# Moving the query transposes of an attention loop to other places, two weight transposes to an earlier place, and two loads to an earlier step

## The chip, the core and the metric

The kernel runs on one core of one Trainium2 chip. TensorE (PE) multiplies and transposes, with its weight loads (PEld) running beside it; VectorE (DVE), ScalarE (ACT) and GpSimd (POOL) do the elementwise work, and SyncE (SP) issues most DMA transfers; ACT issues some as well. The metric is the device time of one execution in microseconds (us), as the median of several runs. The profile is one further execution, taken by the hardware profiler.

## The reference

The reference computes the forward output of one transformer-like block and the gradients of all eight inputs, for 2 batches of 4000 tokens with 144 channels, in bf16. One branch is attention with one head, the other a gated convolution with 5 taps:

```python
xa = _layernorm(x, axis=-1)
q, k, v = split(einsum('btd,de->bte', xa, w_qkv))
p = softmax(einsum('btd,bsd->bts', q, k) * D ** (-0.5))
glob = einsum('btd,de->bte', einsum('bts,bsd->btd', p, v), w_att_out)
h = gelu(einsum('btd,de->bte', xa, w_mlp_in));  u, g = split(h);  g = _layernorm(g)
gc[t] = sum_i g[t + i - 2] * dw_csgu[i]          # 5 taps
loc = einsum('btd,de->bte', u * gc, w_mlp_out)
m = concat(glob, loc);  m[t] += sum_i m[t + i - 2] * dw_merge[i]
out = x + einsum('btc,cd->btd', m, w_merge)
...
_out, _vjp = jax.vjp(_f, x, w_qkv, ..., w_merge);  _grads = _vjp(grad_out)
```

## The kernel before

The two batches run one after the other. Each goes through three stages; the function names are those of the code.

**Head** (`phase_head`). Tokens come as 32 blocks of 128, in 8 groups of 4. Normalised tokens are transposed into `xaT`. For batch 0 the weights are made ready first: `Weights.heads`, then `Weights.keys`. `Weights.turn` (L1128 to L1142) transposes one weight by PE through a PSUM tile `pt` (four transposes for 144 by 144) and copies it out with two DVE copies. `heads` turns the value weight, makes the tap scales, forms the product `w_voT` and turns the output weight `w_l_s` (`w_lT`). `keys` turns the query and key weights (`w_qT`, `w_kT`) and forms their product `W.M1`. Then `taps` (DVE, L1244 and L1248) and `taps1` (POOL, L1252) scale copies of `w_voT` and `w_lT` into `w_A` and `w_Bz`. `Norm.stats`, `power`, `shift` and `apply` (L1399 to L1432) normalise a group of tokens, by DVE, POOL, DVE, and then ACT and POOL.

**Attention** (`phase_attn`). It runs over 32 rows `i` of 128 queries and, for each, four column pairs `c2` of 1000 keys. Everything here is issued in the order in which the code writes it. For each `c2`:
- `unit` (L1985, L1989) forms scores `pS` for this pair and the gradient products `pD` for the pair before it; ACT takes the exponential of `pS` (L1997), DVE forms `Sm` from `pD` (L1999).
- Then come two *places*, 0 and 1. Place 0 begins with `yz` (L2035), 16 matmuls for the row two back. Each place may have X fills and ends with at most one step of the planner on PE.

An X fill (`xfill`, L2057 and L2058) is a set of 12 matmuls that adds the contribution of two rows (a row pair) to three key blocks. It needs one PSUM bank, which it gives back once the sum is taken out: by DVE for even fills (`acc`, L2073), by ACT and POOL for odd ones (`xs`, L2069 and L2070). There are 11 fills for a row pair, and the table `fills` says at which place each stands. Counted over the 16 places of a row pair, from slot 0 to slot 15, it says: slot 1 does the first halves of fills 0 and 1, and slot 2 the second halves, so that these two hold a bank each from slot 1 to slot 2. Fill 2 stands at the beginning of slot 3, fills 3 to 5 at slots 5, 6 and 7, fills 6 to 10 at slots 9 to 13.

X fills and the planner's steps draw from the same three banks (`Banks`, L1698 to L1716). The next tile always takes the bank that has been closed or handed out longest ago and is not held; if it has not been emptied yet, the writing engine waits.

The planner (`Steps`, L1719 to L1770) holds generators for the convolution branch (`pair(p)`, one for two blocks, and `wgrad(p)`) and for the query transposes (`jit(g)`, one for a group of four rows). A generator yields the kind of its next piece, how many places must pass first, and what else must have been done. Pieces of kind `V` (no PE work) are issued at every place when they are ready, within a budget. Of the ready pieces with PE work only one is issued at a place, the one that has been due longest. Kind `P` is taken at any place; kind `L` is known to the planner too, but no generator of this kernel yields it. The PE pieces are:
- `ph`: two matmuls (L1809, L1810), twice for each pair, taken out by two ACT instructions.
- `put` (L1665, L1667), four transposes, taken out by ACT, and `conv` (L1693, L1694), twelve matmuls, taken out by ACT. Each runs once for `gnC` and once for `dgC`.
- `jit` (L1954 to L1966): POOL collects a small tile `QB`, and then three steps follow, each with four transposes into `pj` (L1965) and one ACT copy (L1966). Their results are the weights of the matmuls of `unit` for the next four rows. A `jit` is started 16 places before its rows, which is slot 0.

**Tail** (`phase_tail`). It runs over `h` from 0 to 20. At even `h`, `turn` transposes, `put` (L2183) stores the last 16 channels into two DRAM tap tensors, and `fill(g)` (L2177 to L2180) reads 80 rows of taps of group `g` back into `r` with two DMAs issued by ACT (L1647). `out_mm(p)` (L2218, L2219) needs these for `p = 2g` and `2g + 1`; it runs at `h = p + 5`. At `h = 15` `spill_ef` takes four banks of sums out, in batch 0 by ACT copies (L2277 to L2279); from `h = 16` on `gr_part` (L2289) uses two of these banks. DMAs signal through eight counters, which are handed out in the order of the program over both issuing engines; a DMA waits for the one that had its counter before.

```python
due = [t for t in self.tasks if t[1] is not None and
       (t[1][0] == 'P' or t[1][0] == 'L' and self.now % 2) and self._ready(t)]
if due:
    self._step(min(due, key=lambda t: t[0]))
self.now += 1
```

Of the kernel before, what the change touches and what calls it, by code (L numbers as in the profile page):

```python
# [14 lines left out]
D = 144  # L15
# [1045 lines left out]
NGR = 8  # L1061
# [59 lines left out]
class Weights:  # L1121
# [94 lines left out]
    def heads(self, pst, ps, stats):  # L1216

        W, tp_, nc = self.W, self.tmp, self.k.nc
        cw = self.cw
        self.WvT = self.turn(W.Wqkv, D, 2 * D, D, "w_vT", pst)  # L1220
        stats()
        pt = pst.tile([128, 3, 16], BF, tag="tp", name="pt")
        for n_ in range(3):
            nc.tensor.transpose(pt[:, n_, 0:5], cw[0:5, n_ * D:n_ * D + 128], W.ident[0:5, 0:5])
            nc.tensor.transpose(pt[0:DR, n_, 6:11], cw[0:5, n_ * D + 128:n_ * D + D], W.ident[0:5, 0:5])
        nc.vector.tensor_copy(W.wm[:, :, 0, :], pt[:, 0:2, 0:5])
        nc.vector.tensor_copy(W.wm[0:DR, :, 1, :], pt[0:DR, 0:2, 6:11])
        nc.vector.tensor_scalar(W.wm[:, :, :, 2], W.wm[:, :, :, 2], 1.0, None, op0=ALU.add)
        wr = self.wr = tp_.tile([128, 2, 2, 5], F32, name="w_wr")
        nc.vector.tensor_copy(wr[:], W.wm[:, :, :, ::-1])  # L1230
        nc.vector.tensor_copy(self.wcf[:, 0, :], pt[:, 2, 0:5])
        nc.vector.tensor_copy(self.wcf[0:DR, 1, :], pt[0:DR, 2, 6:11])
        self.WvoT = self.pads.pop("w_voT")
        self.vo(ps, self.WvoT, W.Wo, self.WvT)
        WlT = self.turn(self.Wl, D, 0, D, "w_lT", pst)
        self.UT = [self.WvoT, WlT]
        self.A = [tp_.tile([128, 2, 5, D], BF, name="w_A%d" % h) for h in range(2)]
# [17 lines left out]
    def keys(self, pst, ps):  # L1255

        W, tp_, nc = self.W, self.tmp, self.k.nc
        c = float(D) ** -0.5
        WqT = self.WqT = self.turn(W.Wqkv, D, 0, D, "w_qT", pst)
        WkT = self.WkT = self.turn(W.Wqkv, D, D, D, "w_kT", pst)  # L1260
        WqTz = self.pads.pop("w_qTz")
        nc.vector.tensor_copy(WqTz[:, :, 112:128], WqT[:, :, 128:D])
        W.M1 = self.k.wp.tile([128, 2, D], BF, name="w_M1")
        self.fused(ps, lambda kt: WqT[:, kt, :], self.two(WkT), c, 0, 128, W.M1[:, 0, :])
        self.fused(ps, lambda kt: WqTz[:, kt, :], self.two(WkT), c, 0, 128, W.M1[:, 1, :])
# [357 lines left out]
class Taps:  # L1623


    L = 2 + NBK * 128 + 2
# [92 lines left out]
class Steps:  # L1719
# [36 lines left out]
    def place(self, tensor=True):  # L1756

        self.left = min(self.left + self.rate, self.most)
        again = True
        while again:  # L1760
            again = False
            for t in sorted(self.tasks, key=lambda t: t[0]):
                if (t[1] is None or t[1][0] == 'V') and self._ready(t):
                    self._step(t)
                    again = True
        if tensor:
            due = [t for t in self.tasks if t[1] is not None and (t[1][0] == 'P' or t[1][0] == 'L' and self.now % 2) and self._ready(t)]
            if due:
                self._step(min(due, key=lambda t: t[0]))
        self.now += 1  # L1770
# [165 lines left out]
def phase_attn(k, W, b, S):  # L1936
# [3 lines left out]
    with ExitStack() as es:  # L1940
# [6 lines left out]
        P, Sm = S.P, S.Sm  # L1947
# [7 lines left out]
        def jit(g):  # L1955
            r = slice(g * 4, g * 4 + 4)
            jt[g] = [xp.tile([128, 4, 128], BF, tag=t_, name=t_) for t_ in ("QTm", "BTm", "QBr")]
            for off, src in ((0, S.Q_t), (32, S.B_t), (64, S.Q_t), (96, S.B_t)):
                nc.gpsimd.tensor_scalar(QB[:, :, off:off + DR], src[:, r, 128:D], 1.0, 0.0, op0=ALU.mult, op1=ALU.add)
            for step in range(3):  # L1960
                yield 'P', 2
                src = (S.Q_t[:, r, 0:128], S.B_t[:, r, 0:128], QB[:])[step]
                pj = ps_f.tile([128, 4, 128], BF, tag="f", name="pj")
                for j in range(4):
                    nc.tensor.transpose(pj[:, j, :], src[:, j, :], id_[:])  # L1965
                nc.scalar.copy(jt[g][step][:], pj[:])  # L1966
# [145 lines left out]
def phase_tail(k, W, b, S, nrm, nxt):  # L2112
# [3 lines left out]
    with ExitStack() as es:  # L2116
# [33 lines left out]
        def load_dh(g):  # L2150
            nc.sync.dma_start(dh[g // 2][:, g % 2 * 4:g % 2 * 4 + 4, :], S.dh_d[:, g * 4:g * 4 + 4, :])
# [25 lines left out]
        def fill(g):  # L2177
            for h in range(2):
                r_ = G["r", h, g] = wk.tile([128, 512], BF, tag="r80_%d" % h, name="r80")
                taps[h].load(r_[0:80, :], g * 512, 512, nc.scalar)  # L2180
# [27 lines left out]
        def turn_dx2(pt, hT):  # L2208
            nc.scalar.copy(hT[:], pt[:])
# [62 lines left out]
        def spill_ef():  # L2272
            if fin_:
                return fin_.ef(EF)
            EFs = pp.tile([128, 12, D], F32, name="EFs")
            for n_ in range(3):
                nc.scalar.copy(EFs[:, n_ * 3:n_ * 3 + 3, :], EF[n_][:, 0:3 * D].rearrange("p (a b) -> p a b", b=D))  # L2277
            nc.scalar.copy(EFs[:, 9:10, :], EF[3][:, 0:D].rearrange("p (a b) -> p a b", b=D))
            nc.scalar.copy(EFs[0:80, 10:12, :], EF[3][0:80, D:3 * D].rearrange("p (a b) -> p a b", b=D))  # L2279
            nc.sync.dma_start(k.A.EF_d[:, 0:10, :], EFs[:, 0:10, :])  # L2280
            nc.sync.dma_start(k.A.EF_d[0:80, 10:12, :], EFs[0:80, 10:12, :])
# [19 lines left out]
        NPR = NBK // 2  # L2301
        with tc.manual_schedule():
            loads(0)
            load_dh(0)
            load_dh(1)
            loads(1)
            rows80(0)
            prep(0)
            for h in range(NPR + 5):
                g, hf = divmod(h, 2)  # L2310
                if 0 < h < NPR:
                    turn_dx2(*turn_dx(h))
                if hf == 0 and 0 <= g - 2 < NGR - 1:
                    fill(g - 2)
                if h == NPR + 1:
                    fill(NGR - 1)
                if hf == 0 and g < NGR:
                    turn(g, 0)
                    corr(g, 0)
                    turn(g, 1)  # L2320
                    corr(g, 1)
                elif g < NGR:
                    if g:
                        corr(g, 2)
                    corr(g, 3)
                if h == 0:
                    turn_dx2(*turn_dx(0))
                    corr(0, 2)
                if hf == 1 and g + 1 < NGR:
                    rows80(g + 1)  # L2330
                if 0 <= h - 1 < NPR:
                    sums_act(h - 1)
                    sums_dve(h - 1)
                if hf == 0 and g < NGR:
                    put(g)
                if nrm:
                    for lag, f_ in ((5, nrm.apply), (4, nrm.shift), (3, nrm.power), (2, nrm.stats), (1, nrm.load)):
                        q, m = divmod(h - lag, 2)
                        if m == 0 and 0 <= q < NGR:
                            f_(q)  # L2340
                    if NPR + 2 <= h < NPR + 4:
                        narrow_go(k, nxt, h - NPR - 2, nrm.ld)
                if h == NPR - 1:
                    spill_ef()
                if fin_ and 4 <= h < NPR - 1:
                    fin_.loads(h - 4)
                if hf == 0 and g + 1 < NGR:
                    prep(g + 1)
                if 0 <= h - 1 < NPR:
                    means(h - 1)  # L2350
                if 0 <= h - 2 < NPR:
                    fin(h - 2)
                if h == NPR + 4:
                    spill_gr()
                if 0 <= h - 5 < NPR:
                    out_mm(h - 5)
                if fin_ and h == NPR + 4:
                    fin_.gr_out()
                if NPR <= h < NPR + 4:
                    for q in range(4):  # L2360
                        j = (h - NPR) * 8 + 2 * q
                        gr_part(range(j, j + 2))
                        if fin_:
                            fin_.step((h - NPR) * 4 + q)
                if h < NPR:
                    dx_mm(h)
                if hf == 0 and 0 <= g - 1 < NGR:
                    load_x(g - 1)
                if nrm and NPR - 2 <= h < NPR + 1:
                    take_go(k, nxt, 1, h - NPR + 2, nrm.ld)  # L2370
                if hf == 1 and g + 2 < NGR:
                    load_dh(g + 2)
                    loads(g + 2)
# [346 lines left out]
```

## Time and profile before

| | us |
|---|---|
| median of 7 runs | 1271.89 |
| lowest and highest | 1269.64, 1280.3 |
| the profiled execution | 1275.91 |
| its span | 1274.0 |
| PE busy / DVE / ACT / POOL | 1209.3 / 960.7 / 843.4 / 559.2 |

In the span, the head of batch 0 takes from 0 to about 48 us, its attention from 48 to about 545, its tail to about 640. Batch 1's attention begins near 658 and ends near 1155, and its tail runs to the end. Over 48 to 584 us PE is busy for 518.29 of 536 us, DVE for 418.22, ACT for 369.75, POOL for 232.97. PE's busy time counts overlapping matmuls, so that the distance from the start of one matmul to the start of the next says more: it is 0.06 us in a stream of 144 columns.

### The profile page before, as it was taken

Reading aid. Unit: us, or ns where it says so; the run is one execution under the profiler, and the core shown is the slowest. Engines: PE = TensorE matmul, PEld = TensorE weight load, DVE = VectorE, ACT = ScalarE, POOL = GpSimd, SP = SyncE. Lnnn points to the kernel's source line nnn. Section 1 sums busy time; section 2 is a strip of 40 time slices with the busy share of each in tenths; the row PEclk is TensorE's granted clock in tenths of the full one; section 3 lists DMA queues with packets and bytes.
Section 4 is the critical chain, followed back from the end, with each engine's and each line's share of the span. In section 5 each row is a group of like instructions: output and inputs, shape, how many; then the busy total and the mean of one; then the engine's idle time right before and its main releaser. Section 6 shows DMA issues by size and latency. Waiting matters only on the chain.

```text
span 1274.0 us, 39810 instructions
## 1 busy us (share of the span) xinstructions
PE 1209.3 (95%) x15118; PEld 948.8 (74%) x15118; DVE 960.7 (75%) x3261; ACT 843.4 (66%) x2494; POOL 559.2 (44%) x1007
## 2 busy tenths in 40 slices
PE   7999999999999999989999999999999999998995
PEld 4667777777777777789886777777777776778984
DVE  6567788888788787858646678888888878885674
ACT  4767777777777666556567777777767776654442
POOL 6313444454445443357512254544544445225650
PEclk9999999999999999999999999999999999999998
DMA  6479998888999999978857998999898999997861
GB/s 192 115 135 171 144 165 155 159 146 154 171 162 153 157 164 162 153 202 230 223 158 139 156 158 144 157 166 165 149 168 153 159 163 156 159 161 189 254 160 25
DMA packets 633616, 205.43 MB, mean 161 GB/s; under 512 B 576719, under 2 KB 630948, under 8 KB 633380
## 3 DMA queue, kind: packets, MB, share of 16 engines
q1 hardware_dynamic: 626912, 197.46, 82.6%
q10 hardware_dynamic: 6500, 5.32, 1.7%
q8 instruction: 120, 1.97, 0.6%
q14 instruction: 84, 0.69, 0.2%
HBM read 46.11 MB, written 21.79 MB: 53 GB/s over the span
## 4 chain that ended last, share of the span: by engine, by line
PE 69%; DVE 15%; DMA 5%; issue 4%; ACT 4%; POOL 2%; SPq 1%; ACTq 0%; DVEq 0%; POOLq 0%
PE y L2035 15%; PE pS L1989 9%; PE X L2057 8%; PE X L2058 8%; PE pD L1989 7%; DVE Sm L1999 5%; PE pS L1985 5%; PE pb L1518 3%; PE pc L1693 2%; DVE jg L1916 2%; PE po L2218 1%; DMA gs<-in_grad_out_dram 1%; PE gr L2289 1%; DVE acc L2073 1%; DMA dhr<-dh_d 1%
## 5 line engine op out<-in xcount | busy, mean ns | idle before, releaser
L1999 DVE SCALAR_TENSOR_TENSOR Sm<-pD,Pm 128x500 bf16<-128x500 f32 x512 | 325.7, 673 | 83.1 <-PE pD L1989 49.2
L1997 ACT ACTIVATE Pm<-pS 128x500 bf16<-128x500 f32 x512 | 295.9, 586 | 39.4 <-PE pS L1989 36.3
L2057 PE MATMUL X<-Qs,Sm 128*128 128x144 bf16 x2048 | 285.8, 226 | 9.3 <-DVE acc L2073 8.9
L2070 POOL TENSOR_TENSOR acc<-xs,acc 128x432 f32<-128x432 f32 x150 | 169.0, 1127 | 281.2 <-ACT xs L2069 280.8
L2058 PE MATMUL X<-Bt,Pm 128*128 128x144 bf16 x2048 | 285.6, 226 | 0.8 <-DVE Bt L2022 0.8
L2058 PEld LDWEIGHTS <-Pm 128*128 128x128 bf16 x2048 | 200.2, 98 | 11.9 <-issue 11.4
L2057 PEld LDWEIGHTS <-Sm 128*128 128x128 bf16 x2048 | 200.1, 98 | 1.6 <-issue 1.0
L2035 PEld LDWEIGHTS <-PT 128*128 128x128 bf16 x2048 | 137.3, 98 | 31.3 <-issue 3.5
L2035 PEld LDWEIGHTS <-ST 128*128 128x128 bf16 x2048 | 136.4, 98 | 27.6
L2069 ACT COPY xs<-X 128x432 f32<-128x432 f32 x150 | 78.0, 520 | 111.7 <-PE X L2058 103.0
L2073 DVE TENSOR_TENSOR acc<-X,acc 128x432 f32<-128x432 f32 x180 | 104.0, 578 | 54.1 <-PE X L2058 53.5
L1997 ACT ACTIVATION_READ_ACCUMULATOR Pm<-pS 128x1 f32 x512 | 104.8, 205 | 0.0
L1985 PE MATMUL pD<-rb,QBr 16*128 16x500 bf16 x448 | 95.7, 378 | 4.0 <-DVE Sm L1999 3.5
L1989 PEld LDWEIGHTS <-BTm 128*128 128x128 bf16 x512 | 49.9, 98 | 60.2 <-issue 2.1
L1985 PE MATMUL pS<-rb,QBr 16*128 16x500 bf16 x448 | 91.9, 379 | 0.3
L1916 DVE SCALAR_TENSOR_TENSOR jg<-gnC,dgC 128x256 bf16<-128x256 bf16 x160 | 90.0, 562 | 1.2
L2045 POOL TENSOR_TENSOR B_t<-zd,yd 128x144 bf16<-128x144 f32 x64 | 34.1, 532 | 113.3 <-ACT zd L2044 112.9
L1989 PEld LDWEIGHTS <-QTm 128*128 128x128 bf16 x512 | 29.0, 97 | 72.4 <-issue 72.4
L1989 PE MATMUL pS<-rb,QTm 128*128 128x500 bf16 x256 | 76.9, 382 | 0.0
L1989 PE MATMUL pS<-ra,QTm 128*128 128x500 bf16 x256 | 76.5, 380 | 0.0
L2035 PE MATMUL y<-ra,PT 128*128 128x144 bf16 x1024 | 74.9, 227 | 1.4 <-ACT zd L2044 1.4
L2035 PE MATMUL y<-rb,PT 128*128 128x144 bf16 x1024 | 74.3, 226 | 1.4 <-ACT zd L2044 1.4
(638 smaller groups left out, 2878.0 us busy)
## 6 DMA issues: line engine op xcount, KB each, us to landing
gs<-in_grad_out_dram SPq DMA_DIRECT2D x24, 720.0 KB
dh_d<-dh SPq DMA_DIRECT2D x32, 144.0 KB
dhr<-dh_d SPq DMA_DIRECT2D x16, 288.0 KB
gs<-in_grad_out_dram SPq DMA_DIRECT2D x8, 540.0 KB
xg<-in_x_dram SPq DMA_DIRECT2D x21, 144.0 KB
dug_d<-dug SPq DMA_DIRECT2D x16, 144.0 KB
dug<-dug_d SPq DMA_DIRECT2D x32, 72.0 KB
ug_d<-ug SPq DMA_DIRECT2D x32, 72.0 KB
```

The costliest lines, as they stand in the source:

```text
L1518: nc.tensor.matmul(pb[:], goT[:, i * 128 + m:i * 128 + m + 128], W.GL[:, m, :, :].rearrange("p a b -> p (a b)"), start=(m == 0), stop=False)
L1916: nc.vector.scalar_tensor_tensor(jg[:], a_[:, m:m + 256], 1.0, d_[:, 2:258], op0=ALU.mult, op1=ALU.mult, accum_out=dws[:, p, m:m + 1])
L1985: nc.tensor.matmul(o_[h][:, 0:SC], jt[i // 4][2][rr, i % 4, :], S.XR[c2][rr, 0:SC], start=True, stop=False)
L1989: nc.tensor.matmul(o_[h][:, 0:SC], jt[i // 4][w][:, i % 4, :], S.xaT[:, c0:c0 + SC], start=False, stop=True)
L1997: nc.scalar.activation(P[:, pb, c1:c1 + SC], o_[h][:, 0:SC], ACT.Exp, accum_out=ld8[:, 0, n_:n_ + 1])
L1999: nc.vector.scalar_tensor_tensor(Sm[:, pb, c1:c1 + SC], o_[h][:, 0:SC], 1.0, P[:, pb, c1:c1 + SC], op0=ALU.mult, op1=ALU.mult, accum_out=l ...
L2035: nc.tensor.matmul(y[:, w, :], src[:, jj, :], S.xaa[:, j, :], start=(j == 0), stop=(j == NBK - 1))
L2057: nc.tensor.matmul(X[:, jj, :], Sm[:, i % NP, j * 128:(j + 1) * 128], Qs[:, i % 4, :], start=(kk == 0 and jj == 0), stop=False, skip_group ...
L2058: nc.tensor.matmul(X[:, jj, :], P[:, i % NP, j * 128:(j + 1) * 128], Bt[:, i % 4, :], start=False, stop=(kk == 1), skip_group_check=True)
L2069: nc.scalar.copy(xs[:, 0:nj, :], X[:, 0:nj, :])
L2070: nc.gpsimd.tensor_tensor(a_, xs[:, 0:nj, :], a_, op=ALU.add)
L2073: nc.vector.tensor_tensor(a_, X[:, 0:nj, :], a_, op=ALU.add)
```

## The change

There are four edits in three groups.

1. `jit` yields its three steps as kind `L` with 1 place to pass, where they were kind `P` with 2. Kind `L` is now taken at slots 3 to 15 (`self.now % 16 > 2`), where it was at odd places.
2. The query and key weights are turned in `heads`, between the product `w_voT` and the turn of the output weight; `keys` finds them there.
3. In the tail the last two `fill`s, groups 6 and 7, stand together at `h = 15`, just before `spill_ef`. They stood at `h = 16` and `h = 17`.

```diff
@@ Weights.heads
         self.WvoT = self.pads.pop("w_voT")
         self.vo(ps, self.WvoT, W.Wo, self.WvT)
+        self.WqT = self.turn(W.Wqkv, D, 0, D, "w_qT", pst)
+        self.WkT = self.turn(W.Wqkv, D, D, D, "w_kT", pst)
         WlT = self.turn(self.Wl, D, 0, D, "w_lT", pst)
@@ Weights.keys
-        WqT = self.WqT = self.turn(W.Wqkv, D, 0, D, "w_qT", pst)
-        WkT = self.WkT = self.turn(W.Wqkv, D, D, D, "w_kT", pst)
+        WqT, WkT = self.WqT, self.WkT
@@ Steps.place
-            due = [... (t[1][0] == 'P' or t[1][0] == 'L' and self.now % 2) and self._ready(t)]
+            due = [... (t[1][0] == 'P' or t[1][0] == 'L' and self.now % 16 > 2) and self._ready(t)]
@@ jit
             for step in range(3):
-                yield 'P', 2
+                yield 'L', 1
@@ phase_tail
-                if hf == 0 and 0 <= g - 2 < NGR - 1:
+                if hf == 0 and 0 <= g - 2 < NGR - 2:
                     fill(g - 2)
-                if h == NPR + 1:
-                    fill(NGR - 1)
...
                 if h == NPR - 1:
+                    fill(NGR - 2)
+                    fill(NGR - 1)
                     spill_ef()
```

The lines below the first edit keep their order but have numbers higher by one in the profile of the changed kernel (L1965 becomes L1966, L2057 becomes L2058, and so on).

More of the change, by code (lines that the diff above doesn't have):

```diff
@@ L1766, in place @@
         if tensor:
-            due = [t for t in self.tasks if t[1] is not None and (t[1][0] == 'P' or t[1][0] == 'L' and self.now % 2) and self._ready(t)]
+            due = [t for t in self.tasks if t[1] is not None and (t[1][0] == 'P' or t[1][0] == 'L' and self.now % 16 > 2) and self._ready(t)]
             if due:
```

## The prediction

> **What bounds the kernel now.** I read the page first: busy shares, then the chain that ended last, then the costliest groups.
>
> ```profile
> PE 1209.3 (95%) x15118; PEld 948.8 (74%) x15118; DVE 960.7 (75%) x3261; ACT 843.4 (66%) x2494; POOL 559.2 (44%) x1007
> ...
> PE 69%; DVE 15%; DMA 5%; issue 4%; ACT 4%; POOL 2%; SPq 1%; ACTq 0%; DVEq 0%; POOLq 0%
> ...
> L2057 PE MATMUL X<-Qs,Sm 128*128 128x144 bf16 x2048 | 285.8, 226 | 9.3 <-DVE acc L2073 8.9
> ```
>
> PE is busy for 95% and carries 69% of the chain, so only work of PE, or waits of PE, can be gained. The last line shows such a wait: the X fills stand for 8.9 us behind DVE's sums `acc`. The chain of waits, for PE alone, gives (engine, line waited with, cause: total, times, longest):
>
> ```profile
> PE X L2057 <- DVE acc L2073: 8.9, 12, 1.7
> ...
> PE pt L1137 <- DMA w_l_s<-in_w_mlp_out_dram: 3.0, 1, 3.0
> ...
> PE ph L1809 <- ACT dgC L1669: 2.8, 2, 1.4
> ...
> PE po L2219 <- DMA r<-u: 1.9, 1, 1.9
> ...
> PE pc L1693 <- ACT gc L1867: 1.8, 2, 0.9
> ...
> PE ph L1809 <- DVE acc L2073: 1.0, 2, 0.5
> ```
>
> The lines with `acc`, `dgC` and `gc` have one cause. PE's timeline at the longest `acc` wait:
>
> ```profile
> 446.95 0.23 PE L2058 MATMUL X<-Bt,Pm 128*128 128x144 bf16 x1
> 447.01 0.39 PE L1965 MATMUL pj<-w_ident,Q_t 128*128 128x128 bf16 x4
> 449.11 0.22 PE L2057 MATMUL X<-Qs,Sm 128*128 128x144 bf16 x1 [1.71 <-DVE acc L2073]
> ```
>
> This is slot 2 of a row pair. Fills 0 and 1 hold two of the three banks until here. The `jit` step takes the third; fill 2 then gets the bank of fill 0, which ended just before. DVE empties it at 449.05 (448.45 + 0.60) because it does `Sm` (0.67 us from 447.85) first, and PE stands still.
>
> **The change part by part: the planner.** I went through all 117 PE steps of a batch, taking the excess of the gap after (or before) the step over the usual 0.06 us from start to start. `d` is the time from the last start of fill 1 to the end of fill 0's `acc`, per row pair 0.5 to 2.1 us, mean 0.92. Steps that stall fall in three classes; the other places show no stall.
>
> - Slot 2, third bank taken: `jit` 0.26, 0.54, 0.92, 0.86, 0.26, 1.87, `put` 0.56, `ph` 0.71, `conv` 0 = 5.98. The rows fit d − 0.24 for four transposes, d − 0.19 for `ph`, d − 0.66 for the longer `conv`.
> - Slot 3 with slot 2 empty: fill 2 has the third bank, the step gets that of fill 0: `ph` 0.67, `conv` 0.25 and 0 = 0.92. The rows fit d − 0.76.
> - Slots 0 and 1 both: the second step wants the bank of the first, which ACT has not emptied (the `dgC` and `gc` lines): 1.06 + 1.55 = 2.61.
>
> Together 9.51 us in batch 0 and 9.53 in batch 1; the steps of `jit` cause 4.71 of it in each.
>
> Then I ran the planner's rules by hand for the new code. The queue of steps is the same, so every step that `jit` leaves free at slots 0 to 2 is taken by `ph`, `put` or `conv`, which move up by as much as six places. The new places by number (slot = number modulo 16):
>
> - `jit` at 19, 20, 21; 51, 52, 53; 83, 87, 88; 116, 117, 119; 147, 149, 151; 179, 180, 181; 213, 214, 216: one at least at slot 3 in five of seven groups.
> - Slots 0 and 1 both: none, so 2.61 goes.
> - Slot 2: `conv` 0.43, 0.35, 0, 0, `put` 0.26, `ph` 0.61 = 1.65. `jit` has left slot 2, but others stand there.
> - Slot 3 without slot 2: `jit` 0, 0.02, 0.40, 0.14, `ph` 0.67, `conv` 0.18 and 1.34 = 2.75 (3.10 in batch 1, one `d` differs).
>
> The new sum is 4.40 and 4.75, so the gain is 5.1 + 4.8 = **9.9 us**. The steps keep their number and work, 4 transposes and one ACT copy for each `jit` step; only the cover changes. ACT's copies move with them; ACT is busy for 69% (370 of 536 us) of the attention and tail stretch. The tiles turned out here are weights of the next four rows, at least seven places later: no wait there. The DMA transposes that feed those places land at least 3.6 us before their use, more than the phase shrinks in a row pair.
>
> Bounds. Below: if none of the steps now at slots 2 and 3 costs anything (DVE early in each), the gain is the whole 9.5 per batch, 19. Above: the formulas give a new sum of about 13d − 8.3 if every `d` is alike (four `conv`, two others at slot 2, seven at slot 3). It is 9.5, no gain at all, at d = 1.37, and 19 at d = 2.1, the worst row: 19 us lost over two batches. I take the rows' own `d` for each pair, since DVE's work before fill 0's `acc` is not moved by the change.
>
> **The head.** PE stands until 8.40 for `w_l_s`, and only then turns it, and the query and key weights (8 transposes, 1.38 us). In the changed order these 8 go ahead, into the 3.04 us for which PE waits. Their four DVE copies and `w_qTz` follow, and `w_A` on DVE, at 10.68 now, could start at 9.39: at most 1.29 us earlier. But after that POOL bounds the stage:
>
> ```profile
> 9.25 1.39 POOL L1252 TENSOR_TENSOR w_A<-w_lT,w_wr 128x720 bf16<-128x720 bf16 x1 [1.97 <-DVE w_lT L1139]
> 10.73 1.17 POOL L1437 TENSOR_SCALAR g<-gs 128x320 bf16<-128x320 bf16 x1
> ...
> 13.60 1.39 POOL L1252 TENSOR_TENSOR w_A<-w_lT,w_wr 128x720 bf16<-128x720 bf16 x1
> 15.14 0.19 POOL L1413 TENSOR_SCALAR ve<-mv 128x4 f32<-128x4 f32 x1 [0.15 <-DVE mv L1406]
> ```
>
> POOL's row is full from 9.25 to 14.99, and `ve` waits only 0.15 us for DVE: if POOL's row keeps its end, 0.15 is all. But `g` takes 1.17 us while DVE does `w_A`, where elsewhere the same takes 0.46, so POOL may end earlier when DVE is done earlier. I take **−0.6**, near the middle of 0 and −1.29, as both ends are argued from rows equally near. If the weights come late, nothing is lost: they were used at the same place before.
>
> A rule that speaks against this edit: the Trainium skill, page "SBUF — State Buffer", section "Who interferes with whom", says that a DVE instruction with two SBUF inputs contends with a GpSimd instruction that reads SBUF, one locking out the other. The row of `g` (1.17 beside DVE's `w_A`, against 0.46) agrees with it. By it, moving `w_A` ahead only moves the collision onto POOL's own `w_A` at 9.25: the gain would be the 0.15 alone, and the sum smaller by 0.45.
>
> **The tail.** The edit moves four DMAs of ACT's queue (y6, u6, y7, u7) ahead of `spill_ef`. Rows of batch 0:
>
> ```profile
> 622.53 0.32 ACTq L1647 DMA_DIRECT2D r<-y  x1
> ...
> 623.11 1.33 ACT L2277 COPY EFs<-EF 128x432 f32<-128x432 f32 x3
> ...
> 625.64 0.32 ACTq L1647 DMA_DIRECT2D r<-u  x1
> ```
>
> Now y6 is issued, the five copies (1.8 us) run, and u6 goes at 625.64, held back by its counter; PE's `po` waits 1.85 us for it at 629.39. After the edit y6 to u7 come in sequence and the copies behind them. u7's counter is that of a gradient load of SP (L1107), issued at 621.31 and landed at 625.57. So ACT stands until about 625.6, and behind it stand the copies, and behind those PE's `gr`, which uses the two banks that they empty: it starts at 624.68 now and about 626.6 then, 1.9 later. Its gain is the 1.85 wait, which goes as u6 is issued earlier. SP is touched as well: its second load of the last token group takes a counter of a load that lands at 625.74 (issue now 623.61); DVE's statistics end some 2.1 us later, `og` near 630.8, ahead of `out_mm(13)` at 632.22: covered. Net −1.85 + 1.9, I take **+0.1**; ends −1.85 (PE finds `out_mm` work while `gr` waits) and +2.0 (the `po` wait stays behind other transfers). In batch 1 no wait stands at these places: 0, give or take 0.5, the largest slack missed.
>
> Sum: −9.9 − 0.6 + 0.1 = −10.4. The profiled execution takes 1275.91 us (span 1274.0) and would take 1265.5. It lies 4.0 above the median of the runs; the waits counted here don't depend on that, so the median goes from 1271.89 to **1261.5**.
>
> **The rivals.**
>
> - *The new places cost nothing* (DVE early, as at those of the 117 steps without a stall): the whole 19 goes, with 0.5 of the other edits: about 1252.5. For it: four of the new slot 3 rows are priced under 0.2. Against: `d` of 1 to 2 us in row pairs 3 to 7 and 12.
> - *PE runs ahead into the next engine.* Row pairs shortened by 0.3 to 0.7 us each leave DVE (418 of 536 us busy) and ACT less time, and PE meets `pD` behind `Sm`, already 5.9 us in 24 waits, and `y` behind `zd`, 2.7. If half the gain returns so, −5: 1267.
> - *The change doesn't do what it says.* The bank rule, not the kind of step, makes the stall; what moves into slots 0 to 3 costs as much as what leaves. Then 1272. For it: thirteen priced steps stand at slots 2 and 3, against twelve before. Against: those are mostly `conv`, whose 12 matmuls cover 0.66 us of `d`.
> - *Slower: DVE's backlog at fill 0.* If more ACT and DVE work of convolution steps, up to six places earlier, falls ahead of fill 0's `acc`, `d` rises in all row pairs. At 1.37 the planner's gain is gone; from about 1.62 (3.2 us more for each batch) the kernel is slower by 0.5%; at 2.1 it is 1272 + 19, about 1291. For it: row pair 12 has 2.1 already, and `V` pieces follow their `ph` directly. Against: DVE is 78% busy there, and only one `d` of sixteen exceeds 1.5.
>
> **How the numbers follow.** A difference of about 0.5%, 6.4 us, is what a measurement of this kernel can tell from none. The forecast has 0.52 (own range 1258 to 1266, from the head and tail bounds and half of the priced rows), nothing-costs 0.12, running into DVE and ACT 0.17, no effect 0.08, backlog 0.11. Faster is below 1265.5: 0.52 and 0.12, with a little of the third for the forecast's own edge above it: 0.66. Same: 0.23. Slower, above 1278.3: 0.11. The range leaves out half of nothing-costs at the lower end, and at the upper a part of no effect and the backlog, together 0.2: 1253 to 1273.
>
> **What the profile after would show.** The wait of X for `acc` falls from 8.9 to between 2 and 4 us; the lines `ph` behind `dgC` and `pc` behind `gc` vanish; waits of `pj`, `ph` and `pc` for `acc`, at slot 3, rise to about 5 in all. Each attention phase is shorter by about 5 us. In the head `w_A` on DVE starts between 9.4 and 10.6, and no `pt` of the query weight follows `w_l_s`. In the tail `po` no longer waits for `r`, and the `EFs` copies start near 625.6 less the shift. I would be wrong if waits of `pD` for `Sm` grow by over 4 us, if `d` rises over 1.37, or if the steps fall at other places than I worked out.

## The result and the profile after

The changed kernel takes 1281.54 us in the median against 1274.97 us of the kernel before in the same runs: a ratio of 1.0053 with a 95% interval of 1.0039 to 1.0068, so 5.0 to 8.7 us slower. The forecast was 1261.5 us, faster. The profiled execution takes 1286.7 us, with a span of 1284.9 us against 1274.0. It is slower than each of the 14 timed ones (1277.42 to 1284.52), so what is read from it below adds up to more than the median lost.

The page of the changed kernel, first the busy shares, then the clock that PE was granted in 40 slices of the span, then the chain that ended last:

```profile
PE 1222.2 (95%) x15118; PEld 954.5 (74%) x15118; DVE 972.7 (76%) x3261; ACT 841.0 (65%) x2494; POOL 557.1 (43%) x1007
...
PEclk9999999999999999899899999999999999999998
...
PE 69%; DVE 17%; DMA 4%; ACT 4%; issue 4%; POOL 1%; SPq 0%; ACTq 0%; DVEq 0%; POOLq 0%
```

The clock before:

```profile
PEclk9999999999999999999999999999999999999998
```

PE still bounds the kernel, and DVE's share of the chain has gone from 15% to 17%. Two slices in the middle have an 8 where there was none: PE had less than its full clock there.

PE's waits in the changed kernel (total, times, longest):

```profile
PE pD L1986 <- DVE Sm L2000: 11.9, 31, 2.6
PE X L2058 <- DVE acc L2074: 6.9, 8, 1.2
PE gr L2290 <- ACT EFs L2278: 3.7, 1, 3.7
...
PE pc L1694 <- DVE acc L2074: 1.7, 4, 0.6
...
PE ph L1810 <- DVE acc L2074: 0.8, 2, 0.4
...
PE pj L1966 <- DVE acc L2074: 0.5, 2, 0.2
```

The lines of `ph` behind `dgC`, `pc` behind `gc` and `po` behind `r` are gone, as forecast, and X waits less for `acc`, 6.9 against 8.9. But all waits for `acc` together are 9.9 us as before (8.9 and 1.0 then; 6.9, 1.7, 0.8 and 0.5 now). `pD` behind `Sm` has doubled, which the prediction had named as a sign that it is wrong (two stops near row 31 are 4.6 of the 6.0 us more), and a wait of `gr` for `EFs` is new. The line of `pD` before:

```profile
PE pD L1985 <- DVE Sm L1999: 5.9, 24, 0.5
```

To see where the time went I cut the execution at four starts of matmuls of `unit` (L1985 and L1989), which come in the same order in all kernels: the first, the 981st (row 30.6 of 32) and the 1013th (row 31.6) of each batch. All in us, from the traces, one profiled execution each:

| kernel | to row 30.6, batch 0 | same, batch 1 | rows 30.6 to 31.6, batch 0 | same, batch 1 | row 31.6 to batch 1 | row 31.6 of batch 1 to PE's last matmul |
|---|---|---|---|---|---|---|
| before | 464.6 | 459.0 | 14.55 | 14.55 | 136.1 | 126.0 |
| after | 465.2 | 459.2 | 20.8 | 20.1 | 139.1 | 122.5 |
| head edit alone | 462.8 | 458.9 | 14.55 | 14.55 | 136.3 | 125.1 |
| planner's edit alone | 465.1 | 459.0 | 20.8 | 19.65 | 136.4 | 122.9 |
| tail edit alone | 462.8 | 459.4 | 14.55 | 14.55 | 140.3 | 124.7 |
| after without tail edit | 463.8 | 459.4 | 19.55 | 21.4 | 135.8 | 122.0 |
| the same, later `dh` (below) | 464.8 | 459.1 | 14.9 | 14.9 | 136.4 | 123.3 |
| steps off slots 0 and 2 | 460.8 | 455.25 | 14.3 | 14.3 | 138.2 | 123.8 |
| steps off slots 2 and 3 to place 160 | 459.1 | 453.5 | 14.9 | 14.9 | 135.5 | 125.9 |

(In some executions, whatever the kernel, the clock is at half near 80 us, which costs 1.8 us in the first column; batch 1 is free of it.) The changed kernel loses in one row per batch, 6.2 and 5.5 us, and in the tail of batch 0. In the 30 rows where 9.9 us were to be won, nothing moved. The last column is shorter by 3 in the kernels with the planner's edit; its last steps come three places earlier there, but that this is the cause is not shown.

### The profile page after: what moved, and what is told of

It reads as the page before. It is cut to its first block, busy times and chain, and to the rows that moved or that the text cites. A ratio compares the mean times of both kernels' runs of the same rounds, so it can differ in the third digit from the quotient of the medians.

```text
span 1284.9 us, 39791 instructions
## 1 busy us (share of the span) xinstructions
PE 1222.2 (95%) x15118; PEld 954.5 (74%) x15118; DVE 972.7 (76%) x3261; ACT 841.0 (65%) x2494; POOL 557.1 (43%) x1007
## 4 chain that ended last, share of the span: by engine, by line
PE 69%; DVE 17%; DMA 4%; ACT 4%; issue 4%; POOL 1%; SPq 0%; ACTq 0%; DVEq 0%; POOLq 0%
PE y L2036 14%; PE pS L1990 9%; PE X L2058 8%; PE X L2059 7%; DVE Sm L2000 7%; PE pD L1990 6%; PE pS L1986 5%; PE pb L1519 3%; PE pc L1694 3%; PE po L2219 2%; PE EF L2194 2%; DVE jg L1917 2%; DVE acc L2074 1%; PE gr L2290 1%; DMA gs<-in_grad_out_dram 1%
## 5 line engine op out<-in xcount | busy, mean ns | idle before, releaser
L2058 PE MATMUL X<-Qs,Sm 128*128 128x144 bf16 x2048 | 284.5, 226 | 7.1 <-DVE acc L2074 6.9
L2058 PEld LDWEIGHTS <-Sm 128*128 128x128 bf16 x2048 | 200.8, 98 | 1.8 <-issue 1.3
L1986 PE MATMUL pD<-rb,QBr 16*128 16x500 bf16 x448 | 100.1, 380 | 8.3 <-DVE Sm L2000 7.8
L1917 DVE SCALAR_TENSOR_TENSOR jg<-gnC,dgC 128x256 bf16<-128x256 bf16 x160 | 93.8, 586 | 0.9
L2025 POOL TENSOR_SCALAR nr<-nd,rl 128x1 f32<-128x1 f32 x64 | 16.8, 263 | 138.7 <-DVE nd L2018 137.9
```

The source lines that it names most:

```text
L1917: nc.vector.scalar_tensor_tensor(jg[:], a_[:, m:m + 256], 1.0, d_[:, 2:258], op0=ALU.mult, op1=ALU.mult, accum_out=dws[:, p, m:m + 1])
L1986: nc.tensor.matmul(o_[h][:, 0:SC], jt[i // 4][2][rr, i % 4, :], S.XR[c2][rr, 0:SC], start=True, stop=False)
L2058: nc.tensor.matmul(X[:, jj, :], Sm[:, i % NP, j * 128:(j + 1) * 128], Qs[:, i % 4, :], start=(kk == 0 and jj == 0), stop=False, skip_group ...
```

## The loss near row 31: DVE stops for a store

DVE's and PE's timelines of the changed kernel at this row (start, duration, and in brackets the idle time before and what ended it), with the issue of the store from SP's queue:

```profile
513.23 0.30 DVE L1877 TENSOR_TENSOR du<-dug,gc 128x288 bf16<-128x288 bf16 x1
518.11 0.71 DVE L1878 TENSOR_TENSOR dh<-du,gp_t 128x288 bf16<-128x288 bf16 x1 [4.58 <-DMA dh_d<-dh]
518.74 0.66 DVE L2000 SCALAR_TENSOR_TENSOR Sm<-pD,Pm 128x500 bf16<-128x500 f32 x1
...
515.38 0.43 SPq L1906 DMA_DIRECT2D dh_d<-dh  x1
...
517.02 0.38 PE L1986 MATMUL pS<-rb,QBr 16*128 16x500 bf16 x1
519.46 0.57 PE L1986 MATMUL pD<-rb,QBr 16*128 16x500 bf16 x1 [2.06 <-DVE Sm L2000]
```

`dh` is a tile of the convolution branch with three buffers. Its last pair writes the buffer whose store to DRAM (`dh_d`) was issued only at 515.38, behind a transpose and another store in SP's queue, and landed at 518.01. DVE stands for 4.58 us, `Sm` behind it, and PE behind `Sm`. In batch 1 the same wait is 5.48 us and PE stands for 2.56. Before, the same instruction followed its store with 0.1 us to spare:

```profile
521.37 0.30 DVE L1876 TENSOR_TENSOR du<-dug,gc 128x288 bf16<-128x288 bf16 x1
521.77 0.31 DVE L1877 TENSOR_TENSOR dh<-du,gp_t 128x288 bf16<-128x288 bf16 x1
...
518.00 0.42 SPq L1905 DMA_DIRECT2D dh_d<-dh  x1
```

(that store had landed at 521.68). The stop of PE has a second price. Windows of the changed kernel (length, then busy time of PE, PEld, DVE, ACT and POOL; the third number from the end is PE's granted clock):

```profile
510.00:516.00 6.00, 6.00 (x75) 4.52 (x74) 3.43 (x11) 4.24 (x14) 2.77 (x6) 1.00 0.80 164
516.00:520.00 4.00, 1.94 (x21) 1.11 (x19) 1.90 (x6) 1.58 (x5) 1.99 (x5) 0.92 0.25 70
520.00:526.00 6.00, 6.00 (x39) 3.97 (x36) 4.03 (x17) 1.97 (x6) 0.26 (x1) 0.50 0.89 103
```

For 6 us after the stop the clock is at half, and PE does 39 matmul records where it did 75 before. Of the 6.2 us lost in these rows the stop is 2.4 (from start to start); the rest, about 3.8, falls in the stretch at half clock.

## The experiments

**Each edit alone.** First the head:

```diff
+        self.WqT = self.turn(W.Wqkv, D, 0, D, "w_qT", pst)
+        self.WkT = self.turn(W.Wqkv, D, D, D, "w_kT", pst)
         WlT = self.turn(self.Wl, D, 0, D, "w_lT", pst)
...
-        WqT = self.WqT = self.turn(W.Wqkv, D, 0, D, "w_qT", pst)
-        WkT = self.WkT = self.turn(W.Wqkv, D, D, D, "w_kT", pst)
+        WqT, WkT = self.WqT, self.WkT
```

> Only the two weight turns are moved. My theory: the first unit of the attention of batch 0 starts 0.7 us earlier, as in the changed kernel (47.86 us against 48.57), and nothing else changes: about 0.7 us faster, too little for the times to tell from no change; POOL's two w_A scalings take about 2.5 us each in place of 1.39, since DVE's w_A now runs beside them. Rival: that lengthening eats the gain, and the first unit stays at 48.6 us.

Ratio 0.9990 (0.9978 to 1.0002), 1272.79 us against 1274.00: no difference that can be told, and 0.6 lies within it. The first unit starts at 47.64 us, but among the executions without a difference in the head it starts anywhere between 45 and 48.6, so this stage says little. I had expected 2.5 us for each of POOL's two scalings; one takes 3.69 and the other stays at 1.39:

```profile
9.24 3.69 POOL L1254 TENSOR_TENSOR w_A<-w_lT,w_wr 128x720 bf16<-128x720 bf16 x1 [2.07 <-DVE w_lT L1139]
13.02 0.46 POOL L1438 TENSOR_SCALAR g<-gs 128x320 bf16<-128x320 bf16 x1
...
14.34 1.39 POOL L1254 TENSOR_TENSOR w_A<-w_lT,w_wr 128x720 bf16<-128x720 bf16 x1
```

The collision has moved from `g` (1.17 before, 0.46 now) to `w_A` (1.39 before, 3.69 now), which is what the Trainium skill, page "SBUF — State Buffer", section "Who interferes with whom", makes of two inputs on DVE beside a read of GpSimd.

Then the planner:

```diff
-  ... t[1][0] == 'L' and self.now % 2 ...
+  ... t[1][0] == 'L' and self.now % 16 > 2 ...
             for step in range(3):
-                yield 'P', 2
+                yield 'L', 1
```

> Only the planner's edit (kind L with 1 place, and the rule of slots 3 to 15). My theory: in the middle of the attention nothing is won, since the 3.3 us for each batch that PE no longer stands at planner steps come back inside unit, at pD behind Sm; near row 31 DVE waits more than 4 us for a store of dh, PE stands more than 2 us behind it, and a stretch at half clock follows, 5 us for each batch: 3 to 10 us slower in all. Rival: the stalls taken away are a true gain, 3.3 us for each batch, and what was lost is the tail's: 5 to 7 us faster.

Ratio 1.0025 (1.0015 to 1.0036), 1278.18 us: slower, at the lower end of my theory; the rival is out. The profiled execution shows the same cut as the changed kernel: nothing in the rows up to 30.6, then 20.8 and 19.65 in place of 14.55.

Then the tail:

```diff
-                if hf == 0 and 0 <= g - 2 < NGR - 1:
+                if hf == 0 and 0 <= g - 2 < NGR - 2:
                     fill(g - 2)
-                if h == NPR + 1:
-                    fill(NGR - 1)
...
                 if h == NPR - 1:
+                    fill(NGR - 2)
+                    fill(NGR - 1)
                     spill_ef()
```

> Only the two tail fills are moved. My theory: ACT waits for the counters of y7 and u7 with the EFs copies behind, PE waits 3 to 4 us for these before gr where it waited 1.85 for r, and a stretch at half clock follows: 3 to 5 us slower, all of it in the tail of batch 0, none in batch 1. Rival: the tail's loss carries the whole 6.8 us of the change or more.

Ratio 1.0006 (0.9995 to 1.0017), 1274.91 us: less than I expected, and less than its profiled execution shows, in which the stretch to batch 1 is 4.2 us longer, PE waits 3.5 us for `EFs` and the clock is at half from about 621.5 to 628. The times allow 2.2 us at most; the rival is out. In the changed kernel the same place looks like this on ACT, then PE:

```profile
628.43 0.31 ACTq L1648 DMA_DIRECT2D r<-y  x1
631.96 0.31 ACTq L1648 DMA_DIRECT2D r<-u  x1
632.32 1.36 ACT L2278 COPY EFs<-EF 128x432 f32<-128x432 f32 x3 [4.80 <-DMA r<-y]
...
632.89 0.40 PE L2290 MATMUL gr<-ra,dhr 128*128 128x144 bf16 x2 [3.75 <-ACT EFs L2278]
```

u7 is issued at 631.96, when the gradient load that holds its counter has landed (631.94); the copies come behind it, and `gr` behind the copies.

Head and planner together, without the tail edit (the two diffs above that belong to them, and nothing of the third):

> The changed kernel without the tail edit (head and planner). My theory: the times of the head and the planner add: 2 to 9 us slower than before, 4 us less than the changed kernel, and PE's 1.85 us wait of po for r is back. Rival, in which the tail carries the whole loss: 5 to 7 us faster than before.

Ratio 1.0033 (1.0020 to 1.0045), 1278.27 us: as my theory has it, though the tail edit's part in the whole is nearer to 2.5 us (1.0053 against 1.0033) than to 4.

**The store of `dh`.** To the last kernel I added one edit: the piece that begins `dh` of a pair waits four more places after `dh` of the pair three back, the one with the same buffer.

```diff
-        yield 'V', 2, aft(("dh", 3)), 1.1
+        yield 'V', 2, (((("dh", p - 3), 4),) if p >= 3 else ()), 1.1
```

> The changed kernel without the tail edit, and the piece that begins dh of pair p waits four places more after dh of pair p - 3, so that its store has landed when DVE writes the same buffer. My theory (the reuse of dh's buffer is what stops DVE and then PE near row 31, and the half clock follows that stop): rows 30.6 to 31.6 take 14.5 to 15 us again in both batches where the kernel without this edit took 19.6 and 21.4; no stretch at half clock near 520 and 1135; 6 to 10 us less than the changed kernel without the tail edit, 1 to 5 us faster than before. Rival (steps moved earlier pile DVE's work up at the end of the attention, and any wait there is as long): those rows stay above 18 us.

Ratio 0.9990 (0.9980 to 1.0001), 1273.03 us. Rows 30.6 to 31.6 take 14.9 us in both batches, and DVE writes `dh` without a wait:

```profile
520.53 0.30 DVE L1877 TENSOR_TENSOR du<-dug,gc 128x288 bf16<-128x288 bf16 x1
520.87 0.34 DVE L1878 TENSOR_TENSOR dh<-du,gp_t 128x288 bf16<-128x288 bf16 x1
```

No stretch at half clock is left at these rows. That is 5.2 us less than without this edit (a little under the 6 I had given), and the whole loss of head and planner is gone. In the two traces these rows alone give 4.6 and 6.5 us, so the profiled executions show more of this loss than the medians. The run also says that the planner's edit, cured of this wait, wins nothing.

**Why nothing was won in 30 rows.** For each kernel I summed, over the first 30.6 rows of batch 1, by how much the distance from start to start exceeds its usual value: at the planner's PE steps, and inside `unit` (its eight matmuls usually span 0.97 us).

| kernel | at planner's steps | inside `unit` | rows to 30.6, batch 1 |
|---|---|---|---|
| before | 9.8 | 11.2 | 459.0 |
| after | 6.0 | 14.9 | 459.2 |
| after without tail edit, later `dh` | 6.0 | 14.7 | 459.1 |
| steps off slots 0 and 2 | 5.3 | 11.9 | 455.25 |
| steps off slots 2 and 3 to place 160 | 4.4 | 11.5 | 453.5 |

In the changed kernel 3.8 us went from the steps and 3.7 came back inside `unit`. The clearest place is row 24.5. Before, PE stood for 1.39 us at a step of slot 1, and DVE did pieces of the convolution branch in that time:

```profile
414.29 0.28 PE L1809 MATMUL ph<-w_i,rb 128*128 128x288 bf16 x1 [1.39 <-ACT dgC L1669]
414.63 0.38 PE L1985 MATMUL pS<-rb,QBr 16*128 16x500 bf16 x1
414.63 0.38 PE L1985 MATMUL pD<-rb,QBr 16*128 16x500 bf16 x1
```

After, no step stands there, PE comes to the next unit early, and DVE has such pieces ahead of `Sm` (PE first, then DVE, then POOL):

```profile
413.04 0.38 PE L1986 MATMUL pS<-rb,QBr 16*128 16x500 bf16 x1
413.84 0.37 PE L1986 MATMUL pD<-rb,QBr 16*128 16x500 bf16 x1 [0.42 <-DVE Sm L2000]
...
414.44 0.37 PE L1986 MATMUL pD<-rb,QBr 16*128 16x500 bf16 x1 [0.21 <-DVE Sm L2000]
...
410.47 1.49 DVE L1917 SCALAR_TENSOR_TENSOR jg<-gnC,dgC 128x256 bf16<-128x256 bf16 x1
...
412.25 0.45 DVE L1849 TENSOR_TENSOR oq<-oq,t 128x576 bf16<-128x576 bf16 x1
412.73 0.46 DVE L1851 TENSOR_TENSOR gp_t<-oq,a__7907 128x576 bf16<-128x576 bf16 x1
413.11 0.67 DVE L2000 SCALAR_TENSOR_TENSOR Sm<-pD,Pm 128x500 bf16<-128x500 f32 x1
...
410.26 1.42 POOL L1845 TENSOR_TENSOR oq<-oq,h_t 128x576 bf16<-128x576 bf16 x1
```

Two starts late by 0.8 and 0.59 us: the 1.39 that was saved is spent again one unit later. At this place about 1.1 us of DVE's lateness is one `jg`, which took 1.49 us beside POOL's `oq` and takes 0.42 in the middle of its 192 executions; so the place shows how a stall comes back, and not that moved pieces alone bring it back.

I took this first for a law (DVE is late, so a stall of PE only moves). Two runs were to test it by the slots. All PE steps kept to slots 3 to 15, jit as kind L with 1 place, with the head edit and the later `dh`:

```diff
-  ... (t[1][0] == 'P' or t[1][0] == 'L' and self.now % 2) ...
+  ... t[1][0] in 'PL' and self.now % 16 > 2 ...
```

> Head edit, the later dh, jit as kind L with 1 place, and now every planner step on PE, not jit alone, is kept to slots 3 to 15. If the banks were what PE lacks in the middle of the attention, the stalls at slot 2 (3.5 us for each batch with jit alone moved) go and the stretch from the first unit to row 30.6 shortens by 2 to 4 us for each batch. My theory: DVE is late there whatever the bank, the same time comes back at pD behind Sm, and that stretch stays within 1 us of 463 and 459 us.

Ratio 1.0161 (1.0139 to 1.0184), 1293.02 us. The rows to 30.6 shorten by 3.2 us in batch 1, but the last step comes at place 285 in place of 266, and the late steps stand one after the other behind their own DMA loads:

```profile
PE pc L1695 <- DMA dgC<-dgC_d: 18.5, 4, 6.5
```

The stretches after row 31.6 grow by 15 us. So in the middle my theory failed: the 3.2 us lie within the 2 to 4 that the banks were to give. There is something to win at the slots, and a rule too narrow pays for it at the end.

Jit as before, with the head edit, but all steps off slots 2 and 3:

```diff
-  ... (t[1][0] == 'P' or t[1][0] == 'L' and self.now % 2) ...
+  ... t[1][0] in 'PL' and self.now % 16 not in (2, 3) ...
```

> Head edit, jit as before (kind P, 2 places), and every PE step kept off slots 2 and 3. The last step comes at place 272 in place of 266. If the steps at slots 2 and 3 are what PE pays for, 3 us or more less to row 25 in each batch; the last six places cost 1 to 3 us for each batch at the end; in all 0 to 6 us faster than before. If DVE is late whatever the slot: no gain to row 25 and 1 to 4 us slower in all.

Ratio 0.9996 (0.9981 to 1.0010), 1272.31 us. To row 25 batch 1 takes 367.15 us against 371.23 with the head edit alone, with the same work done, so 4.1 less; at the end the delayed steps cost it again, some 9 us behind row 31.6 in each batch where I had set 1 to 3.

**DVE's load.** To see whether less work on DVE brings the gain out, I left out three of the five tap sums. The first try skipped the pieces altogether:

```diff
         for m in range(5):
+            if 0 < m < 4:
+                continue
             yield 'V', 1, (), .6
             nc.vector.scalar_tensor_tensor(jg[:], a_[:, m:m + 256], ...
```

> The kernel before, with three of DVE's five tap sums of wgrad left out (96 of the 160 instructions at L1916, some 54 us of DVE's work; the gradients of those taps are not computed). My theory, that DVE's lateness is behind PE's waits for acc and for Sm alike: the stretch from the first unit to row 30.6 shortens by 4 us or more for each batch, and both waits fall by half or more. Rival (the waits come from the order of fixed steps, Sm before acc, not from DVE's load): the stretch stays within 1.5 us.

> As the kernel without the tail edit and with the later dh, with the same three tap sums left out. My theory: with DVE early the stalls at planner steps are small in both orders, and the stretch from the first unit to row 30.6 is within 2 us of that of the kernel before with the same sums left out. Rival: DVE's load was what hid the planner's gain, and this stretch is 3 us or more shorter for each batch than there.

Both are slower by 2.3 and 2.5% (1301.89 and 1303.94 us), with less work. A place has a budget for pieces, and without these pieces others came in their places, several ahead of one `acc`: in the first of the two X waits for `acc` up to 4.5 us. As a test of DVE's load these two failed; they show how much the places of DVE's pieces weigh. The second try left every piece in place and only its instruction out:

```diff
             yield 'V', 1, (), .6
-            nc.vector.scalar_tensor_tensor(jg[:], ...
+            if m in (0, 4): nc.vector.scalar_tensor_tensor(jg[:], ...
```

> The kernel before with the same three of five tap sums left out on DVE (54 us of its work in all), but now every piece of the planner stays at its place: only the instruction is missing. My theory, that PE's waits for acc and for Sm are both DVE's lateness: the stretch from the first unit to row 30.6 shortens from 463 and 459 us by 4 us or more in each batch, and the wait of X for acc falls by half. Rival (fixed order, Sm before acc, not load): the stretch stays within 1.5 us.

> Head, planner's edit and the later dh, with the same instructions missing and every piece at its place. If DVE's load is what gave the planner's gain back, the stretch from the first unit to row 30.6 is now 2 us or more below that of the kernel before with the same instructions missing, in each batch. If the order of DVE's fixed steps gave it back, the two stretches are within 1 us, as they are with all the work in.

One profiled execution each. The kernel before then takes 457.0 us to row 30.6 in batch 1 (2.0 less; X behind `acc` 5.4 against 8.9), with the planner's edit and the later `dh` 455.95 (3.1 less). Both lie between what I had set for the two sides: DVE's load is a part of PE's waits, and about 1.1 us of what the planner's edit takes from the steps comes out when DVE has some 24 us less to do in a batch (960.7 to 913.0 us busy in all). Batch 0 can't be compared, as one of the two has stretches at half clock in it.

**Steps off the costly slots.** Off slots 0 and 2, jit as 'L' with 1 place, head edit, later `dh`; once with the tail fills behind `spill_ef`, once as before:

```diff
+  ... t[1][0] in 'PL' and self.now % 16 not in (0, 2) ...
                 if h == NPR - 1:
                     spill_ef()
+                    fill(NGR - 2)
+                    fill(NGR - 1)
```

> Head, jit as kind L with 1 place, every PE step kept off slots 0 and 2, the later dh, and the two tail fills just behind spill_ef in place of ahead of it. Tail: if ACT's wait for the counters with the EFs copies behind is the cause of the tail's loss, gr does not wait for EFs, po waits about 2 us for r as before, and the stretch from row 31.6 to batch 1 is 136 us or less, against 139 to 140. Middle: no step at slot 2, 14 at slot 3; if only the slot of a step matters, 3 us less to row 25 for each batch, as where all steps kept to slots 3 to 15; if DVE is late whatever the slot, within 1 us of before. In all 2 to 8 us faster than before.

> Head, jit as kind L with 1 place, every PE step off slots 0 and 2, the later dh, the tail fills where they were before. If the middle carries the gain of the run with the fills behind spill_ef: about 0.6% faster than before again, 3 to 4 us for each batch in the stretch to row 30.6. If the fills carried it: within 2 us of before.

Ratios 0.9940 (0.9921 to 0.9960) and 0.9940 (0.9920 to 0.9960), 1265.93 and 1266.10 us. So the fills' place wins nothing, and `gr` does not wait for `EFs` where they stand behind it. The rows to 30.6 of batch 1 take 455.0 and 455.25 us, 3.6 to 3.9 less than with the head edit alone: the stalls fall at the steps (5.0 and 5.3) and rise only to 11.9 inside `unit`. But I had set the test at row 25, with 3 us less there if the slot of a step is all that matters, and there batch 1 takes 371.68 and 371.69 us against 371.23, with one step more done: nothing is won so far. The gain comes whole behind row 25, and why it does is not settled. The stretch from row 31.6 to batch 1 is 137.35 us with the fills behind `spill_ef`, a little over the 136 that I had set.

And off slots 2 and 3, but only up to place 160, jit as before, with the head edit and the later `dh`:

```diff
+  ... t[1][0] in 'PL' and (self.now % 16 not in (2, 3) or self.now > 160) ...
```

> Head, jit as before, the later dh, and every PE step kept off slots 2 and 3 up to place 160 (row 20) and free from there. By row 20 as many steps are done as before (72). If steps at these slots cost PE their stalls for good: 3 us less to row 20 in batch 1, kept to the end (the last step comes at place 264), in all 4 to 8 us faster than before. If the stalls only come back later, in unit behind Sm: no gain by row 30.6.

Ratio 0.9914 (0.9895 to 0.9932), 1263.00 us: 8.7 to 13.4 us faster than before, more than the 4 to 8 that I had set, and the best of all. Batch 1 is at row 20 after 291.67 us, against 295.02 with the head edit alone and the same number of steps done: 3.35 us, and it stays won. At row 30.6 it is 5.4; what the further 2 us come from, where the rule no longer holds, is not shown. The later `dh` was not tried on the steps of before, but to row 25 this run and the last one without it take the same, 367.18 and 367.15 us. PE's waits of this kernel:

```profile
PE pD L1986 <- DVE Sm L2000: 4.9, 20, 0.4
...
PE X L2058 <- DVE acc L2074: 2.7, 2, 1.4
```

X behind `acc` is down from 8.9 to 2.7, no other wait of PE for `acc` is left (9.9 in all before), and `pD` behind `Sm` has not risen from 5.9.

## Why the prediction was wrong

**The cause of the stalls was right.** A step at slots 2 or 3 makes PE pay for DVE's lateness through the banks; the last run wins by avoiding just these. The steps fell at the places that I had worked out.

**The price of the moved steps was too low.** I took each row pair's own `d` "since DVE's work before fill 0's `acc` is not moved by the change". It is moved: the pieces of kind `V` follow their PE steps. In the trace of the changed kernel `d` of the row pairs with the steps at 114, 146 and 162 is 1.59, 1.36 and 1.66 us, against 1.09, 0.50 and 0.80 before, and that with 211 is 1.17 against 2.10. Put into the prediction's own formulas these give 0.93, 1.12, 1.47 and 0.41, close to what the steps cost: the formulas were right and the `d` in them wrong. (The mean of `d` rose only from 0.89 to 1.00 in batch 0, and in the last run it is 0.93, so it is not an earlier DVE that wins there.) Predicted 4.40 us in batch 0, found by the same reading 6.2. The steps at 114, 146 and 162 cost 0.97, 1.13 and 1.40 where I had 0.43, 0.26 and 0.61; 258 cost 0.57 where I had 0; only 211 was cheaper, 0.42 against 1.34.

**What was won came back.** This is the step that failed for the 9.9 us: a stall taken from a step was counted as time won. The rival in which PE runs ahead into the next engine had it right, and I had let it take half. It took all: 3.7 of 3.8 us. Why it is 3.7 here and under 1 with the steps off slots 0 and 2 is not settled. It depends on which of DVE's pieces stand ahead of which `Sm`; I have no rule for that, only the counts.

**The loss was nowhere in my list.** For the moved steps I looked at DMA transposes and at ACT's copies, but not at the buffers of the pieces behind them. The prediction put waits of the moved pieces for a store at nothing, without a reason. The store of `dh` had 0.1 us of slack in the trace of before; a `V` piece moved ahead of it stops DVE for 4.58 and 5.48 us, and the run with the later `dh` shows that this is what made head and planner together slower; the tail edit adds about 2.5 us in the whole. Of the rivals only the backlog of DVE ended on this side, and it named another mechanism.

**The tail had the right chain and the wrong size.** ACT stood for u7's counter, the copies behind it, and `gr` behind the copies. I had taken the landing of the gradient load from the old row, 4.26 us after its issue; it took 6.32 (625.62 to 631.94), with the fills' loads beside it. PE stood for 3.75 us, not 1.9, and half clock followed.

**The head** was within its bounds, at a size that the times can't tell.

## What to carry to other kernels

When a scheduler moves steps, everything that it ties to them moves too: for each such piece look up what last read the buffer that it writes, and how long before it that read, or store, was over; a slack of 0.1 us is a wait in the next version. A stall that goes at one place has to be followed to the next instruction of the same engine that waits for the same other engine, and counted there before it is called a gain. And where a slot is the cost, keep all kinds of steps off it, but not so tightly that the last steps come late.

## What the runs showed of the hardware

Short stops of PE can cost more than their length. In the sixteen profiled executions (before, after and the fourteen runs), from 100 us to 40 us behind the last `unit` of batch 1, there are 37 stops of PE of 2.06 us or more. In 33 of them a stretch at half clock began during the stop or within 2 us of its end, or was already running; four had none (2.07, 2.11, 2.60 and 2.87 us). Of the 25 stops from 1.6 to 2.05 us eleven were followed so and fourteen were not, among them 1.71 us on both sides. None of the 38 from 1.2 to 1.6 us was. So there is no sharp line in these runs. Not every stretch has such a stop ahead: near 286 us, in the two executions with steps off slots 0 and 2, there is none. The Trainium skill, page "TensorE: Matmul & The Clock Gate", section "HAM oscillation — how this bites in real kernels", gives as its rule no idle gaps of PE over about 3.4 us. Here gaps of 2.06 us were followed by half clock, and the measurement decides.

One DVE instruction took 1.49 us (`jg`, row 24.5) where the same takes 0.41 near row 31, and POOL's `w_A` 3.69 where it takes 1.39 in the trace of before: pieces that are moved also meet other neighbours.
